# A memset on VectorE as the signal at the change of array halves, and a maximum in front of the second step

## The chip, the core and the metric

One core of a Trainium2 chip. The metric is the device time of one execution, in microseconds (us). TensorE is called PE in the rows of the profile, VectorE DVE, ScalarE ACT, GpSimd POOL.

## What is computed

```python
xn = _layernorm(x)                                  # 2048 x 512
q, k, v = xn @ wq, xn @ wk, xn @ wv                 # 32 heads of 16; one k and one v for all heads
scores = jnp.einsum("bhqd,bkd->bhqk", q, k) * (Dh ** -0.5)
o = jnp.einsum("bhqk,bkd->bhqd", _softmax(scores), v)
s = o @ wo
h = jnp.einsum("bsd,df->bsf", xn, w1) + b1          # 512 -> 1792
g = _silu(jnp.einsum("bsf,fd->bsd", mish(h), w2))   # 1792 -> 512
return x + s * g
```

Attention with 32 query heads on one key and value head over 2048 positions, and a dense branch (two products with Mish between them) that gates it. All in float32.

## The kernel before

The kernel is one program for all five engines, written out by a loop over 512 steps. It keeps every engine's queue in the order in which the loop issues the work. Nothing reorders it later, and an engine that waits holds back all that stands behind in its queue.

**Attention.** The 2048 queries by 32 heads are cut into 32 units of 16 steps. A step makes four score blocks, each with one matmul `e` (L1098, 128 keys by 512 queries) and one exponential on ScalarE (`pt`, L1100). The maximum of each query's scores must be known before its exponential. So the kernel also forms the scores the other way round, 128 queries by 512 keys, with a matmul `m` (L1119), and VectorE reduces each such block to one column (`mb`, L1123). These run 20 steps ahead; there are about four of them in a step. After every second step stands a block of products of the exponentials with the values (`pv`, L1187), which sums over the keys.

**Two halves of the array.** `e` and `m` contract over 64 rows or fewer and so take one half of TensorE's 128 rows. Two matmuls in different halves run side by side. The dense products (`xps`, issued at L120: the projections and the two layers of the branch) contract over 128 rows. They are split into two half products of 64 rows, so that each has a score or a maximum's matmul for a neighbour. A run of up to eight products (`XMAX`) is done twice: in a first step their one half, in array half `h`, and in the step that follows the other half, in the other array half. Both add into the same PSUM bank. Between the first and the second step there is no `pv` block, and behind the second one there is.

**What sets the order.** `waves` (L691 and on) writes one step. `xs` are the step's half products. `a` holds what runs in the other array half: the four scores and some maxima's matmuls. `b` holds the maxima's matmuls that share the products' half. While `xs` has products, one product and one item of `a` are issued in turn, and `b` mostly comes at the end. A dense result of 12 products makes two runs of six, one of 15 a run of eight and a run of seven.

**The change of halves.** Both steps add into one bank from different array halves, and the kernel orders them. It takes an instruction as `relay`: the exponential (or the maximum) of the first item of `a` that is issued behind the last product of the first step. The second step's first product waits for that instruction (`add_manual_dep`). The last stage of the program (`late_pair`, `lane_part`) has another signal for the same purpose: a memset of one column on VectorE, tile `turns`, that waits for the last product (L638).

**Banks.** The kernel's PSUM pools hold three buffers of a bank each for `e` (`ps_e`), three for `m` (`ps_m`), one for `pv` and one for the dense sums (`ps_x`). They are used in turn, so the matmul of a maximum waits until VectorE has finished the maximum three before it, and a score until ScalarE has finished the exponential three before it. In runs of odd length one maximum's matmul takes a bank of `ps_e`.

Of the kernel before, what the change touches and what calls it, by code (L numbers as in the profile page):

```python
# [126 lines left out]
def block_kernel(ctx: ExitStack, tc: tile.TileContext, x, wq, wk, wv, wo, w1, b1, w2, out):  # L127
# [10 lines left out]
    pe, act, dve, pool, sp = nc.tensor, nc.scalar, nc.vector, nc.gpsimd, nc.sync  # L138

    step = [-10 ** 6]  # L140
    lead = {}
# [411 lines left out]
    def begin():  # L553
        prepare()
        if qqueue and is_ready(qqueue[0]):
            g = qqueue.popleft()
        elif queue and is_ready(queue[0]):
            g = queue.popleft()
        else:
            n = next((n for n, g in enumerate(queue) if g.wo is None), None)  # L560
            if not n or not is_ready(queue[n]) or queue[n].m1 is None:
                return False
            g = queue[n]
            del queue[n]
        if g.start:
            g.start()
        if len(g.mms) == 15 and spare_steps() > 1:
            g.most = 5
        if g.alloc:
            ps = g.alloc()  # L570
        else:
            ps = ps_x.tile([P, 512], F32, tag="x", name="xps")
        cur.update(g=g, n=0, ps=ps, chunk=[], relay=None)
        return True

    def finish():
        g = cur["g"]
        if cur["n"] < len(g.mms):
            return False
        for i in g.items:  # L580
            i.users -= 1
        cur["g"] = None
        evacs[0] += g.dve
        if lead:
            lead["post"](g, cur["ps"])
        else:
            g.post(cur["ps"])
            g.done = step[0]
        return True
# [17 lines left out]
    SYNC = mybir.DependencyInfo(mybir.DependencyClass.Sync, mybir.DependencyReason.DATA)  # L607
    turns = cp.tile([P, 2], F32, name="turns")
# [79 lines left out]
    def chunk_size(n, most):  # L688
        return -(-n // -(-n // most)) if n else 0

    def waves(h, em, new):  # L691

        if not cur["chunk"] and (not new or cur["g"] is None and not begin()):
            mms = []
        else:
            g = cur["g"]
            mms = cur["chunk"] or g.mms[cur["n"]:cur["n"] + chunk_size(len(g.mms) - cur["n"], g.most)]  # L700
        second = bool(cur["chunk"])
        k = len(mms)
        ms = em(k, second)
        a = deque(ms[1 - h])
        b = deque(ms[h])
        ps = cur["ps"]
        ends = second and cur["n"] + k == len(cur["g"].mms)
        xs = deque(mms)
        swap = k % 2 and k > 5 and not second
        relay = None  # L710
        first = True
        done = False
        while a or b or xs:
            if xs:
                i = xs.popleft().half(ps, h)
                if first and cur["relay"] is not None:
                    tc.add_manual_dep(i.ins, cur["relay"].ins.name, mybir.DependencyInfo(
                        mybir.DependencyClass.Sync, mybir.DependencyReason.DATA), reason="other half of the bank")
                first = False
                if ends and cur["g"].dve and len(xs) == HOLD + k % 2:  # L720
                    held[0] = []
                if not xs and ends:
                    cur["n"] += k
                    cur["chunk"] = []
                    finish()
                    done = True
                    for top in held[0] or ():
                        top()
                    held[0] = None
            elif b and not swap:  # L730
                b.popleft()()
            if len(a) > 1 or a and not xs:
                r = a.popleft()()
                if k and not xs and relay is None:
                    relay = r
            if b and swap and not xs and not a:
                b.popleft()()
        if k and not done:
            assert relay is not None
            cur["relay"] = relay  # L740
            if second:
                cur["n"] += k
                cur["chunk"] = []
            else:
                cur["chunk"] = mms
# [620 lines left out]
    for c0, c1 in ((0, 1), (1, 2), (2, 3), (3, 4)):  # L1366
# [4 lines left out]
        for c in range(c0, c1):  # L1371
            xs, scs = [], []
# [71 lines left out]
    def best(eng):  # L1444
        found = None
        for k in plan[eng]:
            s = k.start(T[eng])
            if s is not None:
                rank = max(s, T[eng] + 0.1) + WAIT_US * k.prio
                if found is None or rank < found[2]:  # L1450
                    found = (s, k, rank)
        return found
# [5 lines left out]
    while True:  # L1458
# [7 lines left out]
        b = best("PE")  # L1466
# [89 lines left out]
    for s in range(NS + 2000):  # L1556
        inm = s < NS - LEAD
        if inm or cur["chunk"]:
# [4 lines left out]
            def em(k, second):  # L1563
                n, rest = m_sides(1 - h, k, second) if inm else (0, 0)
                x = deque(lambda i=i: e_one(s, i) for i in range(4))
                y = deque(lambda: m_one(1 - h) for _ in range(n))
                r = [[], []]
                for op in EM if k % 2 == 0 or k == 5 or second else EM[::-1]:
                    if op == "M" and y:
                        r[1 - h].append(y.popleft())  # L1570
                    elif op == "E":
                        r[1 - h].append(x.popleft())
                r[h] = [lambda j=j: m_one(h, n + rest > 4 and j == rest - 1) for j in range(rest)]
                return r

            if s >= 2 and (s - 1) % 16 == 0 and s > 1:
                gap[0] += 1
            waves(h, em, s < NS - LEAD - 1 and s % 2)
            if s % 2 == 0:
                act_jobs(2 + (len(jobs) > 4))  # L1580
# [58 lines left out]
```

## Time and profile before

| | |
|---|---|
| median of 3 runs | 1700.35 us (1698.67 to 1701.35) |
| the profiled execution | 1699.96 us |
| its span, first to last instruction | 1698.0 us |
| PE busy | 1558.2 us, 92% |
| DVE busy | 1331.6 us, 78%, 2331 instructions |
| ACT busy | 1312.2 us, 77% |
| maxima (`mb`, L1123) | 2048, 1267.7 us busy, 683 ns each |
| exponentials (`pt`, L1100) | 2018, 1064.0 us busy, 601 ns each |
| granted TensorE clock | 0.997 |

Rows of the timeline begin with start and duration in us; a row that ends in x8 merges eight instructions that follow each other on the engine. What stands in brackets is the time the engine was idle just before, and what ended that. Rows of the waits give the total in us, the number of times and the longest.

### The profile page before, as it was taken

What the parts mean: (1) busy time and instruction counts of PE and PEld (TensorE: products, weight loads), DVE (VectorE), ACT (ScalarE), POOL (GpSimd) and SP (SyncE); (2) the same over time, 40 slices, a digit from 0 to 9 for tenths busy, and PEclk for the clock granted to TensorE, in tenths of its full rate; (3) what the DMA queues carried; (4) which work ended last, traced back from release to release, by engine and by line L of the source; (5) the groups of instructions that cost most, each with busy time, mean ns of one, the idle gap of its engine ahead of it and who ended that gap; (6) DMA issues with size and microseconds to landing.
All of it is one profiled execution on the core that took longest, in us unless ns stands there. A gap on an engine that the chain in (4) does not pass through costs nothing.

```text
span 1698.0 us, 31802 instructions
## 1 busy us (share of the span) xinstructions
PE 1558.2 (92%) x11738; PEld 885.9 (52%) x11738; DVE 1331.6 (78%) x2331; ACT 1312.2 (77%) x2518; POOL 633.6 (37%) x683
## 2 busy tenths in 40 slices
PE   9999999999999989999999999999999999899998
PEld 5545555555555455555555555555555555555454
DVE  7977787788888777788888877877888887778732
ACT  7677787788887678868888777886887878778777
POOL 5764355363463106403415130371241414125312
PEclk9999999999999999999999999999999999999999
DMA  6223221131331214122022312221322212031011
GB/s 210 71 80 115 85 82 49 59 110 60 116 97 52 78 37 127 42 64 77 24 74 72 99 53 64 75 59 27 107 88 76 72 38 101 17 103 54 14 40 61
DMA packets 74666, 124.31 MB, mean 73 GB/s; under 512 B 21520, under 2 KB 35344, under 8 KB 74512
## 3 DMA queue, kind: packets, MB, share of 16 engines
q1 hardware_dynamic: 74512, 122.29, 23.6%
q8 instruction: 93, 1.52, 0.4%
q14 instruction: 61, 0.50, 0.1%
HBM read 74.78 MB, written 26.21 MB: 59 GB/s over the span
## 4 chain that ended last, share of the span: by engine, by line
PE 69%; ACT 26%; DVE 3%; issue 1%; DMA 0%; SPq 0%; POOL 0%; ACTq 0%; DVEq 0%
PE xps L120 28%; PE pv L1187 27%; ACT pt L1100 25%; PE e L1098 6%; PE m L1119 5%; DVE mb L1123 2%; PE xps L116 0%; PE late L120 0%; ACT os L1196 0%; PE late L1098 0%; DMA xin<-in_dram 0%; ACT t L847 0%; PE kp L351 0%; PE wop L116 0%; PE xp L302 0%
## 5 line engine op out<-in xcount | busy, mean ns | idle before, releaser
L1123 DVE TENSOR_REDUCE mb<-m 128x1 f32<-128x512 f32 x2048 | 1267.7, 683 | 305.3 <-PE m L1119 234.5
L1100 ACT ACTIVATE pt<-e 128x512 f32<-128x512 f32 x2018 | 1064.0, 601 | 332.7 <-PE e L1098 300.3
L1119 PE MATMUL m<-ks,qt 48*128 48x512 f32 (+1 forms) x2048 | 830.3, 423 | 2.9 <-DVE mb L1123 1.8
L1098 PE MATMUL e<-qt,ks 64*128 64x512 f32 x2018 | 741.9, 402 | 0.5 <-ACT pt L1100 0.2
L1187 PE MATMUL pv<-pt,vaug 128*32 128x512 f32 x4096 | 492.9, 599 | 0.0
L1119 PEld LDWEIGHTS m<-ks,qt 48*128 48x128 f32 (+1 forms) x2048 | 372.6, 185 | 58.3 <-DVE mb L1123 18.6
L120 PE MATMUL xps<-wbs,act 64*128 64x512 f32 x1248 | 338.6, 407 | 50.5 <-ACT pt L1100 50.5
L1098 PEld LDWEIGHTS e<-qt,ks 64*128 64x128 f32 x2018 | 373.7, 186 | 20.1 <-ACT pt L1100 8.3
L120 PE MATMUL xps<-xt,ws 64*128 64x512 f32 x1104 | 305.8, 409 | 45.3 <-ACT pt L1100 45.3
L120 PEld LDWEIGHTS xps<-wbs,act 64*128 64x128 f32 x1248 | 217.3, 185 | 180.1 <-ACT pt L1100 99.9
L120 PEld LDWEIGHTS xps<-xt,ws 64*128 64x128 f32 x1104 | 190.1, 184 | 175.7 <-ACT pt L1100 110.4
L1187 PEld LDWEIGHTS pv<-pt,vaug 128*32 128x32 f32 x4096 | 107.0, 109 | 222.3 <-issue 212.9
L174 POOL TENSOR_SCALAR t<-t 128x512 f32<-128x512 f32 x56 | 34.4, 614 | 416.6 <-ACT t L838 416.6
L164 POOL TENSOR_TENSOR hb<-hb,t 128x512 f32<-128x512 f32 x56 | 72.1, 1288 | 110.5 <-ACT t L851 97.2
L120 PE MATMUL xps<-xt,wq 64*128 64x512 f32 x336 | 93.2, 409 | 14.0 <-ACT pt L1100 14.0
L120 PE MATMUL xps<-wbs,ot_all 64*128 64x512 f32 x288 | 79.5, 408 | 11.7 <-ACT pt L1100 11.7
L120 PEld LDWEIGHTS xps<-xt,wq 64*128 64x128 f32 x336 | 58.1, 184 | 52.3 <-ACT pt L1100 33.8
L164 POOL TENSOR_TENSOR hb<-hb,u 128x512 f32<-128x512 f32 x56 | 72.3, 1290 | 4.4
L120 PEld LDWEIGHTS xps<-wbs,ot_all 64*128 64x128 f32 x288 | 49.6, 184 | 45.4 <-ACT pt L1100 27.6
L164 POOL TENSOR_TENSOR u<-u,t 128x512 f32<-128x512 f32 x56 | 71.5, 1277 | 4.7
L164 POOL TENSOR_TENSOR act<-hb,act 128x512 fp32r<-128x512 f32 x55 | 70.5, 1281 | 4.6
L159 POOL TENSOR_SCALAR qh<-qf 128x512 fp32r<-128x512 f32 x15 | 9.3, 620 | 134.1 <-ACT qf L770 134.1
(158 smaller groups left out, 954.1 us busy)
## 6 DMA issues: line engine op xcount, KB each, us to landing
wbs<-w SPq DMA_DIRECT2D x36, 512.0 KB
ws<-w SPq DMA_DIRECT2D x35, 512.0 KB
qt<-qh SPq DMA_DIRECT2D x256, 32.0 KB
w<-wbs SPq DMA_DIRECT2D x14, 512.0 KB
wq<-wq SPq DMA_DIRECT2D x14, 512.0 KB
wbs<-wo SPq DMA_DIRECT2D x12, 512.0 KB
rawws<-in_dram SPq DMA_DIRECT2D x21, 256.0 KB
rawwb<-in_dram SPq DMA_DIRECT2D x20, 256.0 KB
```

The costliest lines, as they stand in the source:

```text
L120: i = self.pe.matmul(ps, self.lhs()[o], self.rhs()[o], start=(self.k == 0 and self.halves == 0), stop=(self.k == self.tot - 1 and self.hal ...
L159: pool.tensor_scalar(o, i, 1.0, 0.0, op0=ALU.mult, op1=ALU.add)
L164: eng.tensor_tensor(out=o, in0=a, in1=b, op=op)
L174: pool.tensor_scalar(o, o, lim, 0.0, op0=ALU.min, op1=ALU.max)
L1098: pe.matmul(e, ks[o:o + 64, P * k:P * (k + 1)], q[o:o + 64, p], start=True, stop=True)
L1100: r = act.activation(pt, e, AF.Exp, scale=0.25)
L1119: pe.matmul(m, q[o, p, P * t:P * (t + 1)], ks[o, C * kb:C * (kb + 1)], start=True, stop=True)
L1123: r = dve.reduce_max(out=mb_of[v][:, kb, z:z + 1], in_=m, axis=AX.X)
L1187: pe.matmul(o[32 * j:32 * j + 32], vaug[:, k], pt, start=(k == 0), stop=(k == 15))
```

## The change

Two things change in `waves`. Behind the last product of a first step a memset of one column of `turns` is issued on VectorE, with a dependency on that product, and it becomes the relay. And a second step begins with one item of `b`, if there is one, in front of its first product.

```diff
         done = False
+        own = second
         while a or b or xs:
-            if xs:
+            if own and b:
+                b.popleft()()
+                own = False
+            elif xs:
                 i = xs.popleft().half(ps, h)
                 if first and cur["relay"] is not None:
                     tc.add_manual_dep(i.ins, cur["relay"].ins.name, mybir.DependencyInfo(
                         mybir.DependencyClass.Sync, mybir.DependencyReason.DATA), reason="other half of the bank")
                 first = False
+                if not xs and not second and not lead:
+                    relay = dve.memset(turns[:, 0:1], 0.0)
+                    tc.add_manual_dep(relay.ins, i.ins.name, SYNC, reason="half of the bank")
                 if ends and cur["g"].dve and len(xs) == HOLD + k % 2:
                     held[0] = []
```

The new program has 243 more instructions on VectorE, one memset for each change of halves, and as many as before on the other engines. Line numbers behind L712 grow by up to 7: the scores stand at L1105, the maxima's matmuls at L1126, the maxima at L1130, the `pv` products at L1194, the new memset at L725.

On TensorE, at a change of halves in a run of six (the words in brackets name the engine's semaphore that a row waits for; `m_0_28` is a maximum's matmul of array half 0, `e_2` the third score of a step), the kernel before has:

```order
L120 MATMUL xps<-xt_216,early 128x512
L1098 MATMUL e_2_2870<-qt_79,ks 128x512 [waits Activation_49]
L1119 MATMUL m_1_27_2874<-ks,qt_77 128x512 [waits DVE_49]
L1098 MATMUL e_3_2877<-qt_79,ks 128x512 [waits Activation_49]
L120 MATMUL xps<-xt_216,early 128x512 [waits Activation_49]
L1119 MATMUL m_1_28_2886<-ks,qt_77 128x512 [waits DVE_49]
L120 MATMUL xps<-xt_216,early 128x512
L1098 MATMUL e_0_2890<-qt_79,ks 128x512
L120 MATMUL xps<-xt_216,early 128x512
L1119 MATMUL m_1_29_2895<-ks,qt_77 128x512 [waits DVE_49]
```

The changed kernel has, at the same place:

```order
L120 MATMUL xps<-xt_216,early 128x512
L1105 MATMUL e_2_2891<-qt_79,ks 128x512
L1126 MATMUL m_1_27_2895<-ks,qt_77 128x512 [waits DVE_49]
L1105 MATMUL e_3_2898<-qt_79,ks 128x512 [waits Activation_49]
L1126 MATMUL m_0_28_2906<-ks,qt_77 128x512 [waits DVE_49]
L1126 MATMUL m_1_28_2909<-ks,qt_77 128x512 [waits DVE_49]
L120 MATMUL xps<-xt_216,early 128x512 [waits DVE_49]
L1105 MATMUL e_0_2913<-qt_79,ks 128x512 [waits Activation_49]
L120 MATMUL xps<-xt_216,early 128x512
L1126 MATMUL m_1_29_2918<-ks,qt_77 128x512 [waits DVE_49]
```

The second step's first product now waits for VectorE's semaphore in place of ScalarE's, and the matmuls of two maxima, `m_0_28` and `m_1_28`, stand in front of it. From there on an item of `a` stands in front of each product, where it stood behind it.

On TensorE, at the end of that second step, the kernel before has:

```order
L1119 MATMUL m_1_30_2904<-ks,qt_77 128x512 [waits DVE_49]
L120 MATMUL xps<-xt_216,early 128x512
L1098 MATMUL e_2_2910<-qt_79,ks 128x512 [waits Activation_49]
L1119 MATMUL m_0_28_2914<-ks,qt_77 128x512 [waits DVE_49]
L1098 MATMUL e_3_2917<-qt_79,ks 128x512 [waits Activation_49]
L1187 MATMUL pv_2566<-pt_0_2854,vaug 32x512
```

and the changed kernel:

```order
L1126 MATMUL m_1_30_2927<-ks,qt_77 128x512 [waits DVE_49]
L120 MATMUL xps<-xt_216,early 128x512
L1105 MATMUL e_2_2931<-qt_79,ks 128x512 [waits Activation_49]
L120 MATMUL xps<-xt_216,early 128x512
L1105 MATMUL e_3_2938<-qt_79,ks 128x512 [waits Activation_49]
L1194 MATMUL pv_2583<-pt_0_2874,vaug 32x512
```

The maximum's matmul `m_0_28` has left the step's end, and the last product stands where it stood, behind the third score. The instruction that reads the finished sum on ScalarE (or VectorE) moves with that product: on ScalarE it now comes behind the third exponential of the step.

On VectorE, through the same first and second step, the changed kernel has:

```order
L1130 TENSOR_REDUCE mb_2273<-m_0_25_2868 128x1 [waits PE_49]
L1130 TENSOR_REDUCE mb_2273<-m_0_26_2877 128x1 [waits PE_49]
L1130 TENSOR_REDUCE mb_2273<-m_0_27_2886 128x1 [waits PE_49]
L725 MEMSET turns 128x1 [waits DVE_49,PE_49]
L1130 TENSOR_REDUCE mb_2273<-m_1_27_2895 128x1 [waits PE_49]
L1130 TENSOR_REDUCE mb_2273<-m_0_28_2906 128x1 [waits PE_49]
L1130 TENSOR_REDUCE mb_2273<-m_1_28_2909 128x1 [waits PE_49]
L1130 TENSOR_REDUCE mb_2273<-m_1_29_2918 128x1 [waits PE_49]
L1130 TENSOR_REDUCE mb_2273<-m_1_30_2927 128x1 [waits PE_49]
```

The memset stands behind the first step's third maximum. `m_0_28` was last of these eight maxima before and is fifth now. In runs of seven and eight `b` is empty in the second step, and only the memset is new there.

## The prediction

> **What bounds the kernel now.** I read the page first: the busy line, then the chain that ended last.
>
> ```profile
> PE 1558.2 (92%) x11738; PEld 885.9 (52%) x11738; DVE 1331.6 (78%) x2331; ACT 1312.2 (77%) x2518; POOL 633.6 (37%) x683
> ...
> PE 69%; ACT 26%; DVE 3%; issue 1%; DMA 0%; SPq 0%; POOL 0%; ACTq 0%; DVEq 0%
> ```
>
> TensorE is idle for 1698.0 - 1558.2 = 139.8 us, and the chain runs through TensorE with a quarter of it on ScalarE. The list of waits says where the two meet.
>
> ```profile
> PE xps L120 <- ACT pt L1100: 127.0, 242, 0.8
> ...
> PE m L1119 <- DVE mb L1123: 1.8, 3, 0.7
> ```
>
> Nearly all of the idle time is one wait: a dense product waits 242 times, 0.52 us each, for an exponential. That is the relay. The kernel has 243 changes of halves; in the program's order I count 174 in runs of six, 30 in runs of eight, 30 in runs of seven and 9 of other lengths. On TensorE hardly anything waits for VectorE. So the change aims at the right row, and the question is what VectorE does at that moment. I take one first and second step in a run of six, near 213 us, on TensorE:
>
> ```profile
> 212.19 0.39 PE L1119 MATMUL m<-ks,qt 48*128 48x512 f32 x1
> ...
> 212.42 0.40 PE L120 MATMUL xps<-xt,early 64*128 64x512 f32 x1
> 212.65 0.43 PE L1098 MATMUL e<-qt,ks 64*128 64x512 f32 x1
> 212.65 0.39 PE L1119 MATMUL m<-ks,qt 48*128 48x512 f32 x1
> 213.56 0.50 PE L120 MATMUL xps<-xt,early 64*128 64x512 f32 x1 [0.48 <-ACT pt L1100]
> 213.56 0.49 PE L1119 MATMUL m<-ks,qt 48*128 48x512 f32 x1
> 213.89 0.39 PE L120 MATMUL xps<-xt,early 64*128 64x512 f32 x1
> ...
> 214.13 0.39 PE L1119 MATMUL m<-ks,qt 48*128 48x512 f32 x1
> ...
> 214.60 0.39 PE L1119 MATMUL m<-ks,qt 48*128 48x512 f32 x1
> ...
> 214.83 0.66 PE L1098 MATMUL e<-qt,ks 64*128 64x512 f32 x2
> 215.06 0.39 PE L1119 MATMUL m<-ks,qt 48*128 48x512 f32 x1
> 215.41 1.92 PE L1187 MATMUL pv<-pt,vaug 128*32 128x512 f32 x16
> ```
>
> The last product of the first step starts at 212.42 and ends at 212.82. The second step's first product starts at 213.56. Matmuls go in pairs, one in each half: from 213.56 to 213.89, 0.33 us behind a wait, then 0.24 apart. Seven pairs lead to the last one at 215.06, a maximum's matmul beside a score, and `pv` follows 0.35 later. VectorE in the same stretch, and ScalarE below it:
>
> ```profile
> 211.72 4.89 DVE L1123 TENSOR_REDUCE mb<-m 128x1 f32<-128x512 f32 x8 [1.23 <-PE xps L120]
> 217.84 0.69 DVE L1123 TENSOR_REDUCE mb<-m 128x1 f32<-128x512 f32 x1 [1.23 <-PE xps L120]
> ```
> ```profile
> 211.93 2.07 ACT L1100 ACTIVATE pt<-e 128x512 f32<-128x512 f32 x4 [1.65 <-PE e L1098]
> ```
>
> The share of 78% hides that VectorE works through eight maxima without a break from 211.72 on and rests only for the 1.23 us around `pv`. One takes 0.69, and the eight end (4.89 - 0.69) / 7 = 0.60 apart: at 212.41, 213.01, **213.61**, 214.21, 214.81 and so on. ScalarE's four end at 214.00, 0.49 apart, so the third, which is the relay, ends at 213.51, and the product starts 0.05 later.
>
> **The change, part by part.** It removes the wait for the exponential. It adds 243 memsets. It moves one maximum's matmul from the last pair to the front of the second step in the runs of six. No DMA moves, and neither does anything on POOL or SP.
>
> *The memset.* It stands behind the third maximum. That one belongs to the matmul at 212.19 and ends at 213.61, after the product has started today. So the signal comes behind a queue and is later than the exponential. The price of the memset, and of its signal, is in the last stage of the program:
>
> ```profile
> 1637.57 0.06 DVE L638 MEMSET turns<- 128x1 f32 x1 [0.16 <-PE e L1098]
> ```
> ```profile
> 1637.11 0.39 PE L120 MATMUL xps<-wbs,act 64*128 64x512 f32 x1
> ...
> 1637.68 0.49 PE L120 MATMUL xps<-wbs,act 64*128 64x512 f32 x1
> ```
>
> It takes 0.06 and the product that waits for it starts 0.05 after its end. With VectorE free, 0.18 us pass from the end of the last product (1637.50) to the next start (1637.68). What it costs in a row of maxima is not in this trace; the nearest rows are those of another small instruction between two maxima:
>
> ```profile
> 372.75 0.68 DVE L1123 TENSOR_REDUCE mb<-m 128x1 f32<-128x512 f32 x1
> 373.34 0.16 DVE L1157 TENSOR_REDUCE mp<-mp 128x16 fp32r<-128x16 f32 x1
> 373.42 1.28 DVE L1123 TENSOR_REDUCE mb<-m 128x1 f32<-128x512 f32 x2
> ```
>
> The reduction of 0.16 moves the next maximum from 373.34 to 373.42, by 0.08. The memset, shorter, costs between 0 and 0.08; I take 0.06, its own length. The Trainium skill, VectorE: DVE Perf Modes, section "The DRAIN you can't avoid", says that the next VectorE instruction starts only when the pipeline of the one before is empty. By that rule the memset would cost its 0.06 and the 0.09 by which two maxima overlap, and the forecast would be 174 x 0.09 = 16 us higher, 1793. The trace disagrees: eight maxima take 4.89 us and not 8 x 0.69 = 5.5.
>
> *The maximum in front.* A matmul `m` takes the bank of the third `m` before it, so it waits for that maximum. That this wait holds the engine is seen once:
>
> ```profile
> 555.24 3.08 DVE L1123 TENSOR_REDUCE mb<-m 128x1 f32<-128x512 f32 x5 [0.60 <-PE m L1119]
> ```
> ```profile
> 555.98 0.50 PE L1119 MATMUL m<-ks,qt 48*128 48x512 f32 x1 [0.55 <-DVE mb L1123]
> 555.99 0.49 PE L1098 MATMUL e<-qt,ks 64*128 64x512 f32 x1
> ```
>
> The first maximum ends at 555.92, the matmul starts at 555.98 (0.05 to 0.06 later), and the score behind it waits too. Before, the three `m` of the second step at 213.56, 214.13 and 214.60 wait for the second, third and fourth maximum (213.01, 213.61, 214.21) and always find them done. With one more `m` ahead of them, each waits for one maximum later. Worked through for this place:
>
> - The maximum in front waits for the second maximum: 213.06, in the old gap.
> - The next `m` waits for the third: 213.61 + 0.05 = 213.66. The product stands behind it and has the memset by then. Today it starts at 213.56.
> - The second pair is 0.33 later, at 213.99.
> - The `m` of the third pair could start at 214.23, but waits for the fourth maximum behind the memset: 214.21 + 0.06 + 0.05 = 214.32. The pair behind a wait again takes 0.33: 214.65.
> - The `m` of the fifth pair waits for the fifth maximum: 214.81 + 0.06 + 0.05 = 214.92. Then 215.25, and the last score 0.24 later, at 215.49.
>
> Today's last pair starts at 215.06: **0.43 us later** for this place. The longer step hides nothing elsewhere: VectorE ends its eight maxima when it did, about 216.6, and only its rest around `pv` grows from 1.23 to 1.7. ScalarE now reads the finished sum behind the third exponential, about 1 us later than today; the next product needs that bank only after `pv`, near 217.7, so `pv` covers it. Without that cover, what ran past would add to the step.
>
> Some steps end late already, because a maximum's matmul was late:
>
> ```profile
> 373.48 0.50 PE L1119 MATMUL m<-ks,qt 48*128 48x512 f32 x1
> 373.57 0.40 PE L1098 MATMUL e<-qt,ks 64*128 64x512 f32 x1
> 373.91 1.07 PE L1187 MATMUL pv<-pt,vaug 128*32 128x512 f32 x8
> ```
> ```profile
> L1154 DVE TENSOR_REDUCE mp<-mb 128x16 f32<-128x64 f32 x32 | 8.5, 266 | 1.1
> ```
>
> This second step begins at 371.88, and its last score starts 1.69 later, where the place above has 1.50. Such steps lie around the 32 changes of unit (the row above counts them); I find 47 among the 174 and give them 0.18 less, 0.25 us. The other 127 get 0.42, a little under the place above, since in some the third maximum ends earlier. Sum for the runs of six: 127 x 0.42 + 47 x 0.25 = 65 us.
>
> *Runs of eight and seven* have nothing in `b`; only the memset takes the relay's place.
>
> ```profile
> 154.10 2.48 DVE L1123 TENSOR_REDUCE mb<-m 128x1 f32<-128x512 f32 x4 [1.34 <-PE m L1119]
> ...
> 161.19 4.28 DVE L1123 TENSOR_REDUCE mb<-m 128x1 f32<-128x512 f32 x7 [1.67 <-PE m L1119]
> ```
> ```profile
> 156.47 0.49 PE L120 MATMUL xps<-wbs,act 64*128 64x512 f32 x1 [0.80 <-ACT pt L1100]
> ...
> 163.08 0.50 PE L120 MATMUL xps<-wbs,act 64*128 64x512 f32 x1 [0.48 <-ACT pt L1100]
> ```
>
> In a run of eight the memset stands behind all four maxima, which end at 154.10 + 2.48 = 156.58. The product comes at 156.63 to 156.69 in place of 156.47: +0.2, 30 times, 6 us. In a run of seven it stands behind the third, at 161.19 + 0.68 + 2 x 0.60 = 163.07; the product comes at 163.12 to 163.18 in place of 163.08: +0.07, 30 times, 2 us. The 9 others at 0.4 make 4 us.
>
> Sum: 65 + 6 + 2 + 4 = +77 us on the profiled execution's 1699.96 (0.39 below the median of the runs): **1777 us, slower by 4.5%**.
>
> **Rivals.** (1) *The signal is early.* The place is the stretch between the last product and the memset. If VectorE had no maxima before it, the product would follow 0.18 behind the last one, the whole 127.0 us could go, and the time would be 1573. It decides at the third maximum: that would have to end by about 212.9, 0.7 before it does. For it speaks the 22% that VectorE is idle; against it that this idle time lies around `pv`, in all three kinds of run. Chance 0.06.
>
> (2) *Weights ahead.* The 0.33 behind a wait might not be paid at short waits, if the next pair's weights are loaded meanwhile. With 0.24 at each place and a free memset the second step is 213.66, 213.90, 214.26, 214.50, 214.86, 215.10, 215.34: +0.28 here, 127 x 0.26 + 47 x 0.09 = 37, with 5 + 1 + 2 for the rest 1745. Against it: pairs behind each kind of wait above take 0.33. Chance 0.13. The Trainium skill, TensorE: Matmul & The Clock Gate, section "The mechanism", says that TensorE pulls a weight load for a row group that isn't in use ahead of running matmuls, which is this rival; no run here shows it behind a wait of 0.1 us.
>
> (3) *The maxima's matmuls find their banks free.* Then only the start moves, 213.56 to 213.66, and one pair goes: 213.66 + 0.33 + 5 x 0.24 = 215.19, +0.13, 23 us, with 8 for the rest 1731. It needs a fourth bank or faster maxima; the rows show neither. Chance 0.04.
>
> (4) *The old wait stays.* The product could wait for both. The order shows VectorE's semaphore alone there, so 0.02, at about 1700.
>
> **How the numbers follow.** The forecast has 0.75, rivals (1) to (4) 0.06, 0.13, 0.04 and 0.02. The forecast alone reaches from 1767 (a memset that costs nothing, 0.06 less in 174 places) to 1787 (one of 0.08, with 0.45 and 0.30 in the runs of six: 71, and 8, 4 and 4 for the rest). The range, 1738 to 1795, takes in rival (2) and a little above that top, and leaves out (1), (3) and (4) with 0.12. A measurement here can tell about 0.2% from no change. Slower: 0.75 + 0.13 + 0.04 = 0.92; same 0.02; faster 0.06.
>
> **What the changed profile would show.** Right: the wait of products for exponentials is all but gone; in its place TensorE waits for VectorE, several hundred times, at the maxima's matmuls of second steps; the memset, 59 ns, starts at the end of a maximum; VectorE's rest around `pv` is 0.3 to 0.4 longer. If second steps begin within 0.2 us of the last product, the place of the memset was misjudged. If they begin where I say but end no later than today, the wait for the banks was.

## The result, and the profile after

The changed kernel takes 1767.71 us (median of 4 runs, 1766.58 to 1767.97), the kernel before 1699.51 in the runs beside it: a ratio of 1.0399, with a 95% interval of 1.0381 to 1.0417. It is 68 us slower. The profiled execution's span grew from 1698.0 to 1765.6 us.

The page after, its busy line and the chain that ended last:

```profile
PE 1679.7 (95%) x11738; PEld 861.5 (49%) x11738; DVE 1328.5 (75%) x2574; ACT 1344.3 (76%) x2518; POOL 633.0 (36%) x683
...
PE 68%; DVE 25%; issue 3%; DMA 2%; ACT 1%; DVEq 0%; SPq 0%; POOL 0%; ACTq 0%
```

The chain has changed its partner: the quarter that lay on ScalarE lies on VectorE. TensorE's busy share rose from 92% to 95% while the kernel became slower. Two things go with that. The matmuls of two maxima now run in the stretch where the product waits and where TensorE stood idle before (215.43 to 216.53 below). And a matmul whose weight load was held is recorded longer (the maxima's matmuls 449 ns on average, 423 before), while a held weight load is not idle time of the matmul rows. In memset_only below, where no maximum is moved, the share is 90%. So the waits stand mostly with the weight loads. Two rows of the list of waits before:

```profile
DVE mb L1123 <- PE m L1119: 234.5, 225, 1.9
...
PEld m L1119 <- DVE mb L1123: 18.6, 52, 1.0
```

and the list after:

```profile
DVE mb L1130 <- PE m L1126: 343.2, 260, 2.6
...
PEld m L1126 <- DVE mb L1130: 182.3, 571, 1.0
...
PEld m L1126 <- DVE turns L725: 73.7, 181, 0.4
PEld xps L120 <- DVE turns L725: 69.7, 61, 1.5
...
PE xps L120 <- DVE turns L725: 47.1, 60, 1.1
```

The wait of products for exponentials on the matmul rows, 127.0 us before, is no longer in the list. The weight loads of the maxima's matmuls now wait 571 times for a maximum, where it was 52 times, and 181 times in a row put down to the memset, about as often as there are runs of six (174). What this load needs is the third maximum, which ends 0.01 before the memset: at the place shown below it starts 0.05 behind that maximum. The first row of each list is the other side of it: VectorE rests longer in front of each new row of maxima.

The same run of six as in the prediction, on TensorE after the change:

```profile
215.43 1.10 PE L1126 MATMUL m<-ks,qt 48*128 48x512 f32 x2
216.06 0.49 PE L120 MATMUL xps<-xt,early 64*128 64x512 f32 x1
...
216.64 0.50 PE L1126 MATMUL m<-ks,qt 48*128 48x512 f32 x1
...
216.98 0.40 PE L1105 MATMUL e<-qt,ks 64*128 64x512 f32 x1
...
217.24 0.49 PE L1126 MATMUL m<-ks,qt 48*128 48x512 f32 x1
...
217.57 0.39 PE L1105 MATMUL e<-qt,ks 64*128 64x512 f32 x1
...
217.81 0.39 PE L1105 MATMUL e<-qt,ks 64*128 64x512 f32 x1
218.13 1.92 PE L1194 MATMUL pv<-pt,vaug 128*32 128x512 f32 x16
```

and on VectorE:

```profile
214.09 2.50 DVE L1130 TENSOR_REDUCE mb<-m 128x1 f32<-128x512 f32 x4 [1.58 <-PE xps L120]
215.93 0.06 DVE L725 MEMSET turns<- 128x1 f32 x1
216.51 2.47 DVE L1130 TENSOR_REDUCE mb<-m 128x1 f32<-128x512 f32 x4
```

and the weight loads of the second step's first pairs:

```profile
216.03 0.18 PEld L1126 LDWEIGHTS m<-ks,qt 48*128 48x128 f32 x1 [0.42 <-DVE turns L725]
216.05 0.18 PEld L120 LDWEIGHTS xps<-xt,early 64*128 64x128 f32 x1
...
216.64 0.18 PEld L1126 LDWEIGHTS m<-ks,qt 48*128 48x128 f32 x1 [0.29 <-DVE mb L1130]
216.64 0.18 PEld L120 LDWEIGHTS xps<-xt,early 64*128 64x128 f32 x1
216.75 0.19 PEld L1105 LDWEIGHTS e<-qt,ks 64*128 64x128 f32 x1
216.75 0.19 PEld L120 LDWEIGHTS xps<-xt,early 64*128 64x128 f32 x1
```

The third maximum ends at 214.09 + 0.69 + 2 x 0.60 = 215.98, the memset at 215.99, and the product starts at 216.06. The two maxima's matmuls in the second step start 0.60 apart (216.64, 217.24), which is VectorE's pace and not TensorE's 0.47 for two pairs. VectorE's rest around `pv` grew from 1.23 to 1.58.

Over all runs of six, eight and seven, I took from the traces the mean time from the first step's first product to the second step's first product, and from there to the first `pv` product (us; 174, 30 and 30 places; the `pv` block is 1.85 in every kernel):

```
kernel                  six          eight        seven
before                  2.42 1.90    2.91 2.07    2.68 1.93
changed                 2.54 2.12    3.14 2.07    2.77 1.88
memset_only             2.54 1.89    3.14 2.07    2.77 1.88
max_first_only          2.52 2.13    2.92 2.07    2.68 1.93
other_bank              2.54 1.89    3.14 2.07    2.77 1.88
memset_early            1.94 2.26    2.54 2.07    2.17 2.44
signal_on_scalar        2.02 2.17    2.51 2.07    2.29 2.31
early_and_max_first     2.53 2.13    2.54 2.07    2.17 2.44
after_half_maxima       2.01 1.84    2.48 2.06    2.24 1.90
before_half_maxima      2.42 1.90    2.91 2.06    2.68 1.88
```

From the first two lines come 174 x 0.338 = 58.8, 30 x 0.232 = 6.9 and 30 x 0.040 = 1.2 us (with unrounded means), 66.9 of the 67.6 us by which the span grew.

### The profile page after: what moved, and what is told of

It is laid out like the page before. It is cut to its first block, busy times and chain, and to the rows that moved or that the text cites. A ratio compares the mean times of both kernels' runs of the same rounds, so it can differ in the third digit from the quotient of the medians.

```text
span 1765.6 us, 32067 instructions
## 1 busy us (share of the span) xinstructions
PE 1679.7 (95%) x11738; PEld 861.5 (49%) x11738; DVE 1328.5 (75%) x2574; ACT 1344.3 (76%) x2518; POOL 633.0 (36%) x683
## 4 chain that ended last, share of the span: by engine, by line
PE 68%; DVE 25%; issue 3%; DMA 2%; ACT 1%; DVEq 0%; SPq 0%; POOL 0%; ACTq 0%
PE pv L1194 26%; DVE mb L1130 23%; PE xps L120 17%; PE m L1126 13%; PE e L1105 10%; DMA wq<-wq 1%; DMA ws<-w 1%; PE xps L116 1%; PE late L120 0%; DVE mp L1161 0%; ACT pt L1107 0%; DVE cr L1173 0%; DMA xin<-in_dram 0%; PE late L1105 0%; PE kp L351 0%
## 5 line engine op out<-in xcount | busy, mean ns | idle before, releaser
L1130 DVE TENSOR_REDUCE mb<-m 128x1 f32<-128x512 f32 x2048 | 1262.5, 683 | 375.4 <-PE m L1126 343.2
L1107 ACT ACTIVATE pt<-e 128x512 f32<-128x512 f32 x2018 | 1095.6, 601 | 367.4 <-PE e L1105 266.3
L1126 PE MATMUL m<-ks,qt 48*128 48x512 f32 (+1 forms) x2048 | 886.4, 449 | 28.0 <-DVE mb L1130 7.2
L1105 PE MATMUL e<-qt,ks 64*128 64x512 f32 x2018 | 736.1, 400 | 0.3
L1126 PEld LDWEIGHTS m<-ks,qt 48*128 48x128 f32 (+1 forms) x2048 | 371.5, 185 | 279.6 <-DVE mb L1130 182.3
L1194 PE MATMUL pv<-pt,vaug 128*32 128x512 f32 x4096 | 493.5, 600 | 0.0
L120 PE MATMUL xps<-wbs,act 64*128 64x512 f32 x1248 | 345.5, 412 | 47.1 <-DVE turns L725 47.1
L1105 PEld LDWEIGHTS e<-qt,ks 64*128 64x128 f32 x2018 | 375.0, 187 | 24.3 <-ACT pt L1107 8.6
L120 PE MATMUL xps<-xt,ws 64*128 64x512 f32 x1104 | 330.2, 427 | 0.0
L1194 PEld LDWEIGHTS pv<-pt,vaug 128*32 128x32 f32 x4096 | 107.2, 109 | 242.0 <-issue 230.5
L120 PEld LDWEIGHTS xps<-xt,ws 64*128 64x128 f32 x1104 | 177.4, 185 | 90.5 <-ACT pt L1107 36.0
L120 PE MATMUL xps<-xt,wq 64*128 64x512 f32 x336 | 102.1, 427 | 0.0
L120 PE MATMUL xps<-wbs,ot_all 64*128 64x512 f32 x288 | 86.2, 427 | 0.0
L120 PEld LDWEIGHTS xps<-xt,wq 64*128 64x128 f32 x336 | 53.8, 185 | 27.6 <-ACT pt L1107 10.9
```

Source lines behind the costliest of these rows:

```text
L120: i = self.pe.matmul(ps, self.lhs()[o], self.rhs()[o], start=(self.k == 0 and self.halves == 0), stop=(self.k == self.tot - 1 and self.hal ...
L1105: pe.matmul(e, ks[o:o + 64, P * k:P * (k + 1)], q[o:o + 64, p], start=True, stop=True)
L1107: r = act.activation(pt, e, AF.Exp, scale=0.25)
L1126: pe.matmul(m, q[o, p, P * t:P * (t + 1)], ks[o, C * kb:C * (kb + 1)], start=True, stop=True)
L1130: r = dve.reduce_max(out=mb_of[v][:, kb, z:z + 1], in_=m, axis=AX.X)
L1194: pe.matmul(o[32 * j:32 * j + 32], vaug[:, k], pt, start=(k == 0), stop=(k == 15))
```

## The experiments

My theory: the signal is late because VectorE reaches the memset only behind its row of maxima, and the maximum in front makes each later one wait one maximum longer for its bank. Rival A: the memset and its signal cost by themselves. Rival B: all comes from the moved maximum.

**memset_only.** The changed kernel with the old order in the second step:

```diff
-        own = second
+        own = False
```

> The changed kernel without the maximum in front: the memset is the relay, the second step is in its old order. Theory (VectorE's queue and the turn of the three banks): the second step's first product starts 0.07 us behind the first step's last maximum, which is 0.12 us later than before in the runs of six (174 places), 0.23 in the runs of eight (30) and 0.04 in those of seven (30); nothing waits for a bank later than before, so the loss is 21 + 7 + 1 = 29 us: about 1729. Rival A (the memset and its signal are the whole cost): as the changed kernel, 1767. Rival B (the signal costs nothing, all comes from the moved maximum): 1700.

Measured: 1724.88 us, beside 1698.81 for the kernel before, ratio 1.0153 (1.0127 to 1.018). That is 26 us slower, where the theory had 29. The list of waits of this kernel shows the wait of old, with the memset in the exponential's place and a little longer:

```profile
PE xps L120 <- DVE turns L725: 153.5, 234, 1.1
```

The start is 0.12, 0.23 and 0.08 us later in the three kinds of run, and the second steps are as long as before or slightly shorter. So neither rival A nor rival B can be the whole cost.

**max_first_only.** The changed kernel without the memset:

```diff
-                if not xs and not second and not lead:
+                if False:
                     relay = dve.memset(turns[:, 0:1], 0.0)
```

> The changed kernel without the memset: the relay is the exponential as before, and a maximum's matmul stands in front of the second step. Theory: in the runs of six the matmul behind it waits for the third maximum, so the product starts 0.10 us later than before, and the third and fifth pair wait for the fourth and fifth maximum as in the changed kernel: about 0.32 us at 174 places, 56 us; runs of seven and eight as before: about 1756, with TensorE waiting for VectorE some 500 times. Rival A (the memset is the cost): 1700. Rival C (the two edits need each other): anything near 1700 or below.

Measured: 1758.56 us, ratio 1.0342 (1.0314 to 1.037): +60, where 56 was expected. Runs of eight and seven are as before to 0.01 us. In the runs of six the start is 0.10 later with no memset anywhere, and the second step 0.23 longer. In its list of waits:

```profile
PEld m L1126 <- DVE mb L1130: 255.3, 745, 1.0
```

Each edit alone costs. Together they cost less than 26 + 60, because the late start in the runs of six (174 x 0.12 = 21 us) is the same time in both.

**after_half_maxima and before_half_maxima.** Both kernels with maxima over half the keys of a block, and with a smaller exponent, so that they leave out half of each maximum and do not give the layer's result:

```diff
-        r = act.activation(pt, e, AF.Exp, scale=0.25)
+        r = act.activation(pt, e, AF.Exp, scale=0.01)
...
-            r = dve.reduce_max(out=mb_of[v][:, kb, z:z + 1], in_=m, axis=AX.X)
+            r = dve.reduce_max(out=mb_of[v][:, kb, z:z + 1], in_=m[:, 0:C // 2], axis=AX.X)
```

> The changed kernel with each maximum taken over 256 of the 512 keys of its block, so that VectorE needs about half the time for it; the scores' exponent is scaled down so that nothing overflows. The output is not the reference's. Theory: with VectorE ahead, the memset runs behind the last product, the second step starts about 0.2 us behind it and no bank is waited for: the changed kernel is then the faster one, about 0.4 us at each change, 1605 (1585 to 1630). Rival A (memset and order cost by themselves, whatever VectorE does): slower than the kernel before with the same maxima, near 1750.

> The kernel before with the same halved maxima and the same scaled exponent. The output is not the reference's. Theory: the second step still waits for the exponential, so little changes, 1692 (1680 to 1700); only the steps that ended late for a maximum's matmul gain. Rival A: the same. The two theories part in the comparison with the changed kernel on the same maxima.

Measured: the changed kernel 1581.26 us, ratio 0.9301 (0.9282 to 0.932); the kernel before 1692.52, ratio 0.9959 (0.9946 to 0.9972). Both ratios are against the kernel before with full maxima. With VectorE out of the way the same change wins 111 us where it lost 68. In the kernel before, with halved maxima, the old wait has not moved:

```profile
PE xps L120 <- ACT pt L1100: 127.3, 242, 0.8
```

In the changed one, at a run of six, VectorE and then TensorE:

```profile
197.15 1.35 DVE L1130 TENSOR_REDUCE mb<-m 128x1 f32<-128x256 f32 x3 [2.37 <-PE m L1126]
198.46 0.06 DVE L725 MEMSET turns<- 128x1 f32 x1
```
```profile
197.85 0.39 PE L120 MATMUL xps<-xt,early 64*128 64x512 f32 x1
...
198.35 0.71 PE L1126 MATMUL m<-ks,qt 48*128 48x512 f32 x2
198.59 0.50 PE L120 MATMUL xps<-xt,early 64*128 64x512 f32 x1
```

The last product ends at 198.24 and the next starts at 198.59, with two maxima's matmuls in between. The memset still comes with the end of the third maximum, 198.50, but that is now 0.26 behind the end of the last product. In the changed kernel with full maxima it was 0.79 (215.19 and 215.98). My expectation of 1605 was 24 us too high: the runs of six and seven gained 0.47 each against the kernel before and those of eight 0.44, where I had about 0.4 at each change, and the halved maxima alone gave 6 us.

**other_bank.** The changed kernel, with the maximum in front in a bank of the scores' pool:

```diff
-                r[h] = [lambda j=j: m_one(h, n + rest > 4 and j == rest - 1) for j in range(rest)]
+                r[h] = [lambda j=j: m_one(h, second and j == 0 or n + rest > 4 and j == rest - 1) for j in range(rest)]
```

> The changed kernel, but the maximum's matmul in front of the second step takes a bank of the scores' pool, so that it doesn't shift the turn of the three banks of the maxima. Theory (turn of the banks): the start of the second step stays 0.12 us late in the runs of six, and of the loss behind it (0.22 us at 174 places) nearly all goes; one score now waits for the fifth maximum, about 0.13 at some places. Together 1725 to 1735. Rival D (the order itself costs: the products come one pair later, whatever bank is used): as the changed kernel, 1767.

Measured: 1726.13 us, ratio 1.0152 (1.0135 to 1.0169), as fast as the kernel with the memset alone. The order of the work is that of the changed kernel; only the turn of the banks differs. Of the 0.22 us by which the second step had grown, nothing is left (1.89 against 1.90 before). In the list of waits those of the maxima's matmuls for a maximum shrink from 182.3 us, and a score waits in their stead, mostly hidden:

```profile
PEld e L1105 <- DVE mb L1130: 42.9, 179, 0.6
...
PEld m L1126 <- DVE mb L1130: 15.3, 37, 1.0
```

Rival D, that the order itself costs, is out.

**memset_early.** As memset_only, but the memset stands in front of the first step's last maximum:

```diff
                 first = False
+                if len(xs) == 1 and not second and not lead:
+                    held[0] = []
                 if not xs and not second and not lead:
                     relay = dve.memset(turns[:, 0:1], 0.0)
                     tc.add_manual_dep(relay.ins, i.ins.name, SYNC, reason="half of the bank")
+                    for top in held[0] or ():
+                        top()
+                    held[0] = None
```

> As the run with the memset alone (no maximum in front), but on VectorE the memset stands in front of the first step's last maximum instead of behind it. Theory: the signal comes 0.6 us sooner, near the end of the second maximum, and the second step starts 0.45 to 0.5 us earlier than before the change; behind it the m matmuls and the last pair wait for VectorE's chain of maxima, so that about 0.17 us remain in the runs of six (30 us), 0.4 in those of eight (13) and 0.25 in those of seven (7): about 1650 (1630 to 1670). Rival A (a memset between maxima costs): slower than before, 1725 as with the memset behind.

Measured: 1664.86 us, ratio 0.9792 (0.9777 to 0.9806): **faster than both kernels**, by 2.1% and 5.8%. Moving one memset past one maximum is worth 60 us against memset_only. The same run of six, on VectorE and on TensorE:

```profile
206.27 1.90 DVE L1135 TENSOR_REDUCE mb<-m 128x1 f32<-128x512 f32 x3 [1.12 <-PE xps L120]
207.51 0.06 DVE L727 MEMSET turns<- 128x1 f32 x1
208.09 2.47 DVE L1135 TENSOR_REDUCE mb<-m 128x1 f32<-128x512 f32 x4
```
```profile
207.64 0.49 PE L120 MATMUL xps<-xt,early 64*128 64x512 f32 x1
207.64 0.50 PE L1131 MATMUL m<-ks,qt 48*128 48x512 f32 x1
...
208.22 0.50 PE L1131 MATMUL m<-ks,qt 48*128 48x512 f32 x1
...
208.82 0.50 PE L1131 MATMUL m<-ks,qt 48*128 48x512 f32 x1
...
209.42 0.50 PE L1131 MATMUL m<-ks,qt 48*128 48x512 f32 x1
```

The memset ends at 207.57, with the second maximum, and the second step starts 0.07 later: 1.94 us behind the first step's start and not 2.42. From there the four maxima's matmuls are 0.60 apart. The step has become a chain on VectorE's pace, and three quarters of the gain are given back in it (2.26 against 1.90). In the runs of seven all of it is (2.17 + 2.44 against 2.68 + 1.93). I had expected 1650, with a gain of 0.25 us left there and 0.17 in the runs of six, where it is 0.12. VectorE's pace in the second step is what is left to attack; that was not tried.

**signal_on_scalar.** As memset_only, with ScalarE for the signal:

```diff
-                    relay = dve.memset(turns[:, 0:1], 0.0)
+                    relay = act.activation(turns[:, 0:1], one, AF.Copy)
```

> As the run with the memset alone, but the signal is a copy of one column on ScalarE, behind the second exponential of the step, in place of the memset on VectorE. Theory (the signal is as late as the queue it stands in): ScalarE reaches it about 0.3 us before the exponential that was the relay, so the second step starts 0.3 us earlier and ends where VectorE's maxima allow: 1655 to 1675. Rival E (any separate signal is dearer than an instruction that is there anyway): 1700 or above.

Measured: 1665.72 us, ratio 0.9794 (0.9774 to 0.9814). A dearer instruction gives the same time as the early memset:

```profile
L725 ACT ACTIVATE turns<-one x243: 192/203/223, 84.5 to 1586.5; 128x1 f32<-128x1 f32 x122
```

It takes 203 ns against the memset's 59, but it stands behind the second exponential and not behind the third maximum, and the second step starts 2.02 behind the first in the runs of six, not 2.54. Rival E, that a separate signal is dear, is out: the place in the queue decides.

**early_and_max_first.** The changed kernel with the early memset, the lines of memset_early added to it.

> The changed kernel with the memset in front of the first step's last maximum. Theory: the signal is early, but in the runs of six the m matmul that now stands in front of the product waits for that last maximum, which ends where it did, so the product gains nothing there and the 0.32 us stay (56 us); runs of eight and seven gain 0.4 and 0.25 (20 us): about 1735. Rival A (the late memset is the whole of it): as fast as the run with the early memset alone, 1650.

Measured: 1748.91 us, ratio 1.0286 (1.0271 to 1.0301), 14 above what the theory gave. In the runs of six nothing changes (2.53 and 2.13): the signal is early and no one can use it, because the matmul in front of the product waits for the last maximum. Against the kernel before, the runs of eight gain 0.37. Those of seven gain nothing, as in memset_early, where 0.25 had been expected; that is about half of the 14. In the list of waits the maxima's matmuls wait for maxima as in the changed kernel:

```profile
PEld m L1131 <- DVE mb L1135: 219.8, 631, 1.0
```

## Why the prediction was right

- **The wait aimed at was the right one, and the signal came later.** Forecast: 0.10 later in the runs of six, 0.2 in those of eight, 0.07 in those of seven. Measured: 0.12, 0.23 and 0.08.
- **Each maximum's matmul waits for one maximum later.** Shown by other_bank, which undoes just that. Forecast for the place near 213 us: the second step's matmuls at 0.66 and 1.26 behind its first product and the last score at 1.83. Measured at the same place: 0.58, 1.18 and 1.75, where before it was 1.50.
- **The term that was mis-sized is the memset in the row of maxima.** I took 0.06 us. Third and fourth maximum end 0.61 apart, 0.60 without it: 0.01. Both later waits of a second step sit behind it. So the place shown loses 0.34 (from first product to `pv`: 4.61 after, 4.27 before) and not 0.43. Of that difference 0.05 is what the memset did not cost, and 0.03 is that `pv` follows 0.32 behind the last score and not 0.35. The product itself starts 0.03 later than I had it, because it waits for the memset; the step's end does not hang on that, since the third pair waits for the fourth maximum.
- **That the runs of six came to 58.8 us, near the 65 of the forecast, is partly luck.** I had 127 places at 0.42 and 47 that end late anyway at 0.25. Place by place, in the program's order, the two traces give 0.33 and 0.36: about 12 us less in the first group, 5 more in the second. That late steps lose less was wrong. Of the 47, 26 lose 0.42 or more. In 25 of these a small reduction starts on VectorE during the second step, and in 1 of the other 21. In the place below it stands in front of the fifth maximum, and the matmul that waits for that maximum starts 0.89 behind the one before it (381.74), where it was 0.60 above:

```profile
381.72 0.26 DVE L1161 TENSOR_REDUCE mp<-mb 128x16 f32<-128x64 f32 x1
```
```profile
382.63 0.49 PE L1126 MATMUL m<-ks,qt 48*128 48x512 f32 x1 [0.16 <-DVE mb L1130]
```

- **The 9 other runs** and all the rest of the span cost under 1 us together, not 4. With the 6.9 and 1.2 of the runs of eight and seven, the sum is 67 and not 77.
- **0.33 behind each wait** held: 216.64 to 216.98, 217.24 to 217.57. Rival (2), weights loaded ahead, did not happen at these waits. The product's weight load at 216.64 is held by no semaphore of its own and goes to the other half, yet it starts with the load in front of it that is held, and the next pair's loads come 0.11 later. The sentence of the Trainium skill (TensorE: Matmul & The Clock Gate, "The mechanism") on pulling loads ahead of running matmuls is seen at work in those next loads, which run at 216.75 beside the matmuls of 216.64. A load that passes a held one is not seen in these rows.
- **Rival (1), the early signal,** decides where the prediction put it, at the third maximum. With halved maxima the change wins, though the product follows 0.35 behind the last one and not 0.18, because the memset still ends with a maximum. With the memset in front of the third maximum it came true in part: the price of 127 us was too high for full maxima, and VectorE's pace behind the start left 35 of it in memset_early.

## What to carry to other kernels

A signal is as early as the queue it stands in. Here its place among the instructions of the engine mattered more than its length (203 ns in the right place beat 59 in the wrong one), and an average busy share of 78% said nothing of the queue at that moment. Work pulled forward into a gap takes its turn of the buffers too, and everything behind it waits for one buffer later; a buffer from another pool can take that away. When a wait is removed, look at which engine's pace the next stretch will then run.

## What the runs showed of the hardware that was not expected

A memset of one column between two maxima costs VectorE 0.01 us and not its 0.06 (208 such places in this trace: the maxima end 611 ns apart by the median, 598 without it). At the place shown it starts at 215.93, 0.05 before the maximum in front of it ends, and the maximum behind it is recorded from 215.90, which is why the row of four takes that one in. The product that waits for the memset starts 0.07 after its end. The Trainium skill (VectorE: DVE Perf Modes, "The DRAIN you can't avoid") says that the next operation does not start until the pipeline is empty, and adds that one which is not held starts earlier. The prediction took the first half for the rule; these rows agree with the second.
